# Linear attention with two feed-forward layers: query and key projections of the first eight head pairs as one group of half-row products

## Chip, cores, metric

The kernel runs on one core of a Trainium2 chip. The metric is device time in microseconds of one execution; several executions are taken and the median is given.

## What is computed

Inputs are q, k, v of shape 4 x 8 x 576 x 64 (batch, heads, tokens, head size), a projection w_phi of 64 x 128, and the weights of two feed-forward layers, 512 x 2048 and 2048 x 512 each. All is float32.

```python
def phi(x):
    proj = np.einsum('bhsd,df->bhsf', x, w_phi)
    proj = proj - np.max(np.abs(proj), axis=-1, keepdims=True)
    return np.concatenate([np.exp(proj), np.exp(-proj)], axis=-1)
q_p, k_p = phi(q), phi(k)
kv  = np.einsum('bhsf,bhsd->bhfd', k_p, v)
z   = np.sum(k_p, axis=2)
num = np.einsum('bhsf,bhfd->bhsd', q_p, kv)
den = np.einsum('bhsf,bhf->bhs', q_p, z)[..., None] + 1e-06
x   = (num / den) with heads joined: 2304 x 512
h = x @ w_in;  x = np.maximum(0.01 * h, h) @ w_out
h = x @ w_in2; x = (h / (1 + np.exp(-h))) @ w_out2
```

## The kernel before

Two heads form a pair: 16 pairs, four to a batch entry. The 64 rows of head 0 lie on partitions 0 to 63, those of head 1 on 64 to 127. The first eight pairs (`full(i)`, `NFULL = 8`) multiply in plain float32, which TensorE does in two passes of weight load and matmul for each product; the other eight split each operand into two fp32r parts. The feed-forward layers follow tile by tile, the first in five tiles of 460 or 462 tokens.

The work of one pair is cut into steps, named in `fns` (L365): `lq` and `lv` load (load_qk L109, load_v L119); `pq0`, `pq1` project the two parts of q (s_pq L205: for full pairs 256 and 320 tokens) with the 64 rows of each head as an operand of its own (L217), into one bank for each head; ScalarE copies them to p (L223, L225) and POOL takes the maximum over partitions into m (L227). `pk0`, `pk1` project 512 tokens of k (s_pk L169), each for two blocks of 128 tokens, on all 128 rows against BDF, a block-diagonal matrix that holds w_phi twice and zeros elsewhere (L180), into one bank each; `pkt` does the last 64 tokens (L195). k_features (L151) takes the maximum (L156), subtracts (L157) and forms both exponentials, negative sign first (L166, L167). `eq0`, `eq1` do this for q (L239, L243, L244). `kv` (s_kv L256) sums features times values, 17 products for the positive and then 17 for the negative sign (L262, L268), and ScalarE copies the bank to KV (L273), of which there is one buffer. `num0`, `num1` (num_full L290; products L302, L305) give numerator and denominator, VectorE divides (L311 to L313), TensorE transposes (L316, L320), and put_x (L282) writes x in two parts.

Each step has a due time within its pair (`OFF0` for full pairs, L370); pairs begin 5 units apart. All steps are sorted by due time, and run_att emits them in that order, between the weight preparation and the feed-forward steps (L719 to L769). The tile framework then places the instructions on the engines' queues: it starts from the emitted order and moves instructions by a simulated time line, as operands and buffers come free, so the order in the trace is not the emitted one. Each engine's queue runs in order.

PSUM has eight banks, four with the tag a and four with the tag y. While the first stage is emitted, the steps pq (two banks each), kv and the transposes take y banks, the others a banks (aps, L61). p, m and qh have two buffers each; a pair uses both, one for each part of q.

The preparation of the feed-forward weights (narrow64, L414) is VectorE and ScalarE work on tiles `raw`, three buffers, loaded on SP's queue (L411) as are q, k and v. The third to twelfth of these loads wait for a token (L409) that POOL writes after the maximum of `pq1` of a given pair (L229, PACE L68). w_phi is loaded by two transfers on ScalarE's queue into wc (L75): first BDF, then wraw (w_phi on both row halves) and the identity.

Of the kernel before, what the change touches and what calls it, by code (L numbers as in the profile page):

```python
# [8 lines left out]
F32 = mybir.dt.float32  # L9
# [10 lines left out]
def tile_linear_attention_ffn_ffn(ctx: ExitStack, tc: tile.TileContext, q, k, v, w_phi, w_in1, w_out1, w_in2, w_out2, out):  # L20


    nc = tc.nc
    B, H, S, D = 4, 8, 576, 64
    F = (w_phi.shape[1] - 128) // 3
# [5 lines left out]
    S0 = 512  # L31
# [6 lines left out]
    NKV, NNUM = 112, 96  # L38
# [5 lines left out]
    gp = ctx.enter_context(tc.tile_pool(name="gp", bufs=2))  # L44
# [7 lines left out]
    def at(shape, dt, tag):  # L52
        return att_pool[0].tile(shape, dt, tag=tag, bufs=AB[0].get(tag, 1), name=tag)

    def ps(tag):

        return psp.tile([128, 512], F32, tag=tag, name=f"ps_{tag}")
# [3 lines left out]
    def aps(step):  # L61

        return ps("y" if PRO[0] and step in ("pq", "kv", "nt") else "a")
# [3 lines left out]
    BDF, wraw, ident = wc[:, 0 : 2 * F].rearrange("p (j f) -> p j f", j=2), wc[:, 2 * F : 3 * F], wc[:, 3 * F :]  # L67
# [5 lines left out]
    def make_consts():  # L73
        for c in (slice(0, 2 * F), slice(2 * F, 3 * F + 128)):
            nc.scalar.dma_start(wc[:, c], w_phi[:, c])  # L75
        first = [const.tile([128, 2], F32, name=f"first{i}") for i in range(2)]
        nc.gpsimd.memset(first[0], 0.0)
        nc.gpsimd.partition_all_reduce(first[1], first[0], 128, bass_isa.ReduceOp.absmax)
# [30 lines left out]
    def load_qk(i):  # L109

        st = P[i]
        st["kr"] = at([128, S0], F32, "kr")
        st["kt"] = at([128, 128], F32, "kt")
        st["qr"] = at([128, S], F32, "qr")
        nc.sync.dma_start(st["kr"], k[i, :, 0:S0])
        nc.sync.dma_start(st["kt"], k[i, :, S0:])
        nc.sync.dma_start(st["qr"], q[i])

# [6 lines left out]
    def sub(out_, x, h):  # L125
        nc.vector.tensor_tensor(out_, x, h.bitcast(F32), op=ALU.subtract)  # L126

    def full(i):
        return i < NFULL
# [21 lines left out]
    def k_features(i, pk, ng, g0):  # L151

        ke = P[i]["ke"]
        km = at([128, 4], F32, "km")
        src = pk[:, 0 : ng * F].rearrange("p (g f) -> p g f", f=F)
        nc.vector.tensor_reduce(km[:, 0:ng], src, op=ALU.max, axis=AX.X, apply_absolute_value=True)  # L156
        nc.vector.tensor_tensor(  # L157
            ke[:, g0 : g0 + ng, 0, :], src, km[:, 0:ng].unsqueeze(2).to_broadcast([128, ng, F]), op=ALU.subtract
        )
        g1 = g0 + ng  # L160
        if g1 == 8:
            return
        if g1 == 9:
            g0 = 4
        e0, e1 = ke[:, g0:g1, 0, :], ke[:, g0:g1, 1, :]
        nc.scalar.activation(e1, e0, AF.Exp, scale=-1.0)  # L166
        nc.scalar.activation(e0, e0, AF.Exp)  # L167

    def s_pk(c2):  # L169
        def f(i):  # L170
            st = P[i]
            if c2 == 0:
                st["ke"] = at([128, 9, 2, F], F32, "ke")
            pk = aps("pk")
            for u in range(2):
                c = 2 * c2 + u
                cs = slice(c * 128, (c + 1) * 128)
                o = pk[:, u * 2 * F : (u + 1) * 2 * F]
                if full(i):
                    nc.tensor.matmul(o, st["kr"][:, cs], BDF.rearrange("p j f -> p (j f)"), start=True, stop=True)  # L180
                    continue
                bh, bl = BDH.rearrange("p j f -> p (j f)"), BDL.rearrange("p j f -> p (j f)")
                nc.tensor.matmul(o, st["krh"][:, cs], bh, start=True, stop=False)
                nc.tensor.matmul(o, st["krl"][:, cs], bh, start=False, stop=False)
                nc.tensor.matmul(o, st["krh"][:, cs], bl, start=False, stop=True)
            k_features(i, pk, 4, 4 * c2)

        return f
# [16 lines left out]
    def s_pq(a):  # L205

        def f(i):
            st = P[i]
            c0, n = part(i, a)
            p = at([128, 2 * n], F32, "p")  # L210
            st["p", a] = p
            pq = [aps("pq"), aps("pq")]
            cs = slice(c0, c0 + n)
            for j in range(2):
                if full(i):
                    r = slice(64 * j, 64 * j + 64)
                    nc.tensor.matmul(pq[j][:, 0:n], wraw[r], st["qr"][r, cs], start=True, stop=True)  # L217
                    continue
                nc.tensor.matmul(pq[j][:, 0:n], WH, st["qs"][:, j, cs], start=True, stop=False)
                nc.tensor.matmul(pq[j][:, 0:n], BDL[:, j], st["qs"][:, j, cs], start=False, stop=True)  # L220
            for j in range(2):
                w = 256 if full(i) else n
                nc.scalar.activation(p[:, j * w : (j + 1) * w], pq[j][:, 0:w], AF.Copy)  # L223
                if w < n:
                    nc.scalar.activation(p[:, 512 + 64 * j : 576 + 64 * j], pq[j][:, w:n], AF.Copy)  # L225
            m = at([128, 2 * n], F32, "m")
            nc.gpsimd.partition_all_reduce(m, p, 128, bass_isa.ReduceOp.absmax)  # L227
            if a == 1 and full(i):
                nc.gpsimd.tensor_copy(token[:, i : i + 1], m[0:1, 0:1])  # L229
            st["m", a] = m  # L230

        return f
# [23 lines left out]
    def s_kv(i):  # L256
        st = P[i]
        ke, va = st["ke"], st["va"]
        pv = aps("kv")[:, 0 : 4 * NKV].rearrange("p (s j d) -> p s j d", s=2, j=2)
        vf = va.rearrange("p c d -> p (c d)")  # L260
        for s in range(2):
            nc.tensor.matmul(  # L262
                pv[:, s, :, 0 : D + 1], ke[:, 8, s, :], va[:, 8:10], start=True, stop=False, skip_group_check=True
            )
            for j in range(2):
                for c in range(4):
                    w = (4 * j + c) * (D + 1)
                    nc.tensor.matmul(  # L268
                        pv[:, s, j], ke[:, 2 * c + j, s, :], vf[:, w : w + NKV], start=False, stop=(j == 1 and c == 3), skip_group_check=True
                    )  # L270
        if full(i):
            st["KV"] = at([128, 2, 2, NNUM], F32, "KV")
            nc.scalar.activation(st["KV"], pv[:, :, :, 0 : NNUM], AF.Copy)  # L273
            return
        h, l = st["KVH"], st["KVL"] = at([128, 2, 2, 2, D], F32R, "KVH"), at([128, 2, 2, 2, D], F32R, "KVL")
        for j in range(2):
            kv_, z_ = pv[:, :, j, 0:D], pv[:, :, j, D : D + 1].to_broadcast([128, 2, D])
            for slot, sr in ((j, kv_), (1 - j, z_)):
                nc.scalar.activation(h[:, j, :, slot, :], sr, AF.Copy)
                sub(l[:, j, :, slot, :], sr, h[:, j, :, slot, :])  # L280
# [68 lines left out]
    def s_fin(a):  # L349
        def f(i):  # L350
            if full(i):
                return
            st = P[i]
            c0, w = part(i, a)
            x = st["x", a]
            nc.vector.tensor_mul(x, x, st["r", a])
            put_x(i, slice(0, 128), x, c0, w)

        return f

    def s_num(a):
        return lambda i: (num_full if full(i) else num_split)(i, a)

    W, WP = 8.0, 5.0
    fns = dict(  # L365
        lq=load_qk, lv=load_v, sp=s_split, pq0=s_pq(0), pq1=s_pq(1),
        pk0=s_pk(0), pk1=s_pk(1), pkt=s_pkt, eq0=s_eq(0), eq1=s_eq(1), kv=s_kv, num0=s_num(0), num1=s_num(1), fin0=s_fin(0), fin1=s_fin(1),
    )
    FIN = 16
    OFF0 = dict(lq=1.1, lv=3.08, sp=3.09, pq0=4.48, pk0=5.33, pk1=5.331, pq1=6.8, eq0=9, pkt=9.13, kv=9.131, num0=11.3, eq1=12.07, num1=16, fin0=11.3001, fin1=16.0001)  # L370
    OFF1 = dict(lv=0.6, lq=-2.1250, sp=0.5, pq0=2.1172, pk0=4.0606, pk1=4.0616, pq1=4.7479, eq0=6.2094, pkt=5.1, kv=8.3898, num0=12.1423, eq1=13.9119, num1=14.457, fin0=FIN, fin1=FIN + 2.3)
    END0 = max(OFF0.values()) + 1
    END1 = max(OFF1.values()) + 1
    ts = [WP * i for i in range(NFULL)]
    ts += [ts[-1] + END0 - min(OFF1.values()) + W * i for i in range(B * HP - NFULL)]
    seq = sorted(((ts[i] + o, i, n) for i in range(B * HP) for n, o in (OFF0 if full(i) else OFF1).items()))
    seq.reverse()
# [337 lines left out]
    def pace(s):  # L715

        return SLOW * min(s, NC) + FAST * max(0, s - NC)

    make_consts()  # L719
    for c in range(PRE):  # L720
        run_att(13.52 + 11.07 * c)
        prep_wi(0, c)
# [52 lines left out]
    for u, gs in GROUPS.items():  # L775
        for i, ps_ in enumerate(gs):
# [7 lines left out]
            if last:  # L784
                y = y3_ops(u, list(ps_))
# [87 lines left out]
```

## Time and profile before

| | |
|---|---|
| median of 3 executions | 964.19 us (962.32 to 964.91) |
| the profiled execution | 963.19 us |
| its span, first to last instruction | 961.4 us |
| PE (TensorE matmuls) busy | 943.6 us, 98% |
| DVE (VectorE) busy | 649.1 us, 68% |
| ACT (ScalarE) busy | 597.2 us, 62% |
| POOL (GpSimd) busy | 78.4 us, 8% |
| transferred | 226.13 MB, 235 GB/s on the mean |

PE is the matmul, PEld the weight load that overlaps it. The end of a matmul is modelled, so groups of matmuls overlap in a listing; the time a group takes of PE is read from its start to the start of the next group. L180 is line 180 of the kernel. "idle before <- releaser" names what ended an engine's idle time.

### The profile page before, as it was taken

The numbers are of one execution on the slowest core, as the hardware profiler recorded it, in microseconds if no ns is written. First come the engines' busy times: TensorE is split into PE (matmuls) and PEld (weight loads), VectorE is DVE, ScalarE is ACT, GpSimd is POOL, SyncE is SP. The second block draws the span as 40 slices with busy tenths as digits, with TensorE's granted clock in tenths as the row PEclk, the third lists the DMA queues.
The fourth block names the chain that finished last, engine by engine and source line by source line (L and its number), as shares of the span: only waits on it lengthen the run. The fifth ranks groups of instructions, "written<-read, shape, count | busy, mean of one in ns | idle before, by whom it ended". The sixth has DMA issues, their size and how long they took to land.

```text
span 961.4 us, 15778 instructions
## 1 busy us (share of the span) xinstructions
PE 943.6 (98%) x5376; PEld 883.6 (92%) x5376; DVE 649.1 (68%) x1279; ACT 597.2 (62%) x1224; POOL 78.4 (8%) x56
## 2 busy tenths in 40 slices
PE   7999999999999999999999999999999999999998
PEld 6878888889999998888888999999999999999998
DVE  6677799986666655278777767778762595624853
ACT  6568687877777776466655556566554565544553
POOL 3434200201111111000000000000000000000000
PEclk9999999999999999999999999999999999999999
DMA  6333477874334232299999999896988778987784
GB/s 223 99 105 102 154 243 256 284 267 129 116 112 116 78 128 79 86 355 384 356 337 334 368 356 346 299 349 239 319 287 294 243 234 264 300 281 222 251 278 138
DMA packets 102384, 226.13 MB, mean 235 GB/s; under 512 B 15008, under 2 KB 24992, under 8 KB 102304
## 3 DMA queue, kind: packets, MB, share of 16 engines
q1 hardware_dynamic: 102016, 224.86, 69.9%
q8 instruction: 43, 0.70, 0.3%
q14 instruction: 37, 0.30, 0.1%
q10 hardware_dynamic: 288, 0.26, 0.1%
HBM read 177.82 MB, written 47.22 MB: 234 GB/s over the span
## 4 chain that ended last, share of the span: by engine, by line
PE 79%; DMA 8%; DVE 6%; ACT 4%; issue 1%; SPq 1%; DVEq 0%; ACTq 0%
PE ps_y L689 18%; PE ps_y L553 16%; PE ps_a L533 16%; PE ps_a L613 10%; PE ps_y L613 8%; DMA d<-rec 2%; PE ps_a L268 2%; PE ps_a L302 2%; DMA rec<-e 2%; PE ps_a L334 1%; PE ps_y L268 1%; DMA raw<-in_moe_w_in_dram 1%; DMA e<-d 1%; PE ps_a L180 1%; DMA w7s<-wst 1%
## 5 line engine op out<-in xcount | busy, mean ns | idle before, releaser
L689 PE MATMUL ps_y<-gt,ws 128*128 128x384 f32 x1008 | 177.2, 337 | 0.0
L689 PEld LDWEIGHTS ps_y<-gt,ws 128*128 128x128 f32 x1008 | 176.4, 188 | 0.1
L553 PE MATMUL ps_y<-gh,wo 128*128 128x460 f32 (+1 forms) x640 | 149.5, 372 | 2.2 <-DVE wo L126 1.3
L553 PEld LDWEIGHTS ps_y<-gh,wo 128*128 128x128 f32 x640 | 119.0, 188 | 16.6 <-ACT gh L429 1.9
L533 PE MATMUL ps_a<-xh,wih 128*128 128x460 f32 (+1 forms) x320 | 119.4, 373 | 0.8 <-ACT p L223 0.8
L533 PE MATMUL ps_a<-xl,wih 128*128 128x460 f32 (+1 forms) x320 | 118.9, 372 | 0.0
L533 PE MATMUL ps_a<-xh,wil 128*128 128x460 f32 (+1 forms) x320 | 118.7, 371 | 0.0
L613 PE MATMUL ps_a<-xs,ws 128*128 128x384 f32 x546 | 104.7, 338 | 0.1
L613 PEld LDWEIGHTS ps_a<-xs,ws 128*128 128x128 f32 x546 | 96.7, 188 | 0.8 <-issue 0.4
L227 POOL PARTITION_ALL_REDUCE m<-p x32 | 72.9, 2280 | 293.7 <-ACT p L223 212.4
L429 ACT ACTIVATE gt<-g 128x384 fp32r<-128x384 f32 x120 | 62.8, 524 | 51.3 <-PE ps_y L689 49.3
L126 DVE TENSOR_TENSOR gt<-g,gt 128x384 fp32r<-128x384 f32 x120 | 66.5, 555 | 34.4 <-ACT gt L429 33.5
L613 PE MATMUL ps_y<-xs,ws 128*128 128x384 f32 x462 | 88.5, 338 | 0.1
L613 PEld LDWEIGHTS ps_y<-xs,ws 128*128 128x128 f32 x462 | 81.7, 188 | 0.6 <-DVE g L589 0.5
L553 PE MATMUL ps_y<-gl,wo 128*128 128x460 f32 (+1 forms) x320 | 81.6, 372 | 0.0
L126 DVE TENSOR_TENSOR gl<-g,gh 128x460 fp32r<-128x460 f32 (+1 forms) x80 | 51.6, 646 | 30.6 <-ACT gh L429 26.1
L533 PEld LDWEIGHTS ps_a<-xh,wih 128*128 128x128 f32 x320 | 60.2, 188 | 7.4 <-ACT p L223 1.0
L553 PEld LDWEIGHTS ps_y<-gl,wo 128*128 128x128 f32 x320 | 60.2, 188 | 7.0
L536 ACT ACTIVATE g<-ps_a 128x460 f32<-128x460 f32 (+1 forms) x80 | 44.1, 552 | 35.9 <-PE ps_a L533 35.1
L533 PEld LDWEIGHTS ps_a<-xh,wil 128*128 128x128 f32 x320 | 60.1, 188 | 6.8
L533 PEld LDWEIGHTS ps_a<-xl,wih 128*128 128x128 f32 x320 | 60.2, 188 | 6.0
L429 ACT ACTIVATE gh<-g 128x460 fp32r<-128x460 f32 (+1 forms) x80 | 46.6, 584 | 8.1 <-PE ps_y L553 7.1
(142 smaller groups left out, 1552.3 us busy)
## 6 DMA issues: line engine op xcount, KB each, us to landing
ws<-w7s SPq DMA_DIRECT2D x336, 256.0 KB, 3.7
wo<-wos SPq DMA_DIRECT2D x64, 512.0 KB, 5.2
w7s<-wst SPq DMA_DIRECT2D x48, 512.0 KB, 6.0
raw<-in_moe_w_in_dram SPq DMA_DIRECT2D x32, 512.0 KB, 5.3
raw<-in_moe_w_out_dram SPq DMA_DIRECT2D x32, 512.0 KB, 5.8
wos<-wo SPq DMA_DIRECT2D x16, 512.0 KB, 4.3
va<-in_v_dram SPq DMA_DIRECT2D x16, 325.0 KB, 4.1
qr<-in_q_dram SPq DMA_DIRECT2D x16, 288.0 KB, 3.9
```

Source lines behind the costliest of these rows:

```text
L126: nc.vector.tensor_tensor(out_, x, h.bitcast(F32), op=ALU.subtract)
L180: nc.tensor.matmul(o, st["kr"][:, cs], BDF.rearrange("p j f -> p (j f)"), start=True, stop=True)
L227: nc.gpsimd.partition_all_reduce(m, p, 128, bass_isa.ReduceOp.absmax)
L268: nc.tensor.matmul(pv[:, s, j], ke[:, 2 * c + j, s, :], vf[:, w : w + NKV], start=False, stop=(j == 1 and c == 3), skip_group_check=True)
L302: nc.tensor.matmul(pb[:, w : w + NNUM], e[:, s, cs], KV[:, s, j], start=(s == 0), stop=(s == 1))
L334: nc.tensor.matmul(o, lhs, st[m, a][:, s, j * w : (j + 1) * w], start=(n == 0), stop=(n == 5))
L429: nc.scalar.activation(h, f, AF.Copy)
L533: nc.tensor.matmul(ph, a[:, kk, :], b_[:, kk, :], start=(m == 0), stop=(m == 3 * KD - 1))
L536: nc.scalar.activation(g, ph, AF.Prelu, alpha=0.01)
L553: nc.tensor.matmul(Y[t][d][:, 0:n], a[:, ds_], b_, start=(c == 0 and m == 0), stop=(c == NC - 1 and m == 1), skip_group_check=True)
L613: nc.tensor.matmul(bank[b_], w[:, a, kk], x[:, c, kk], start=(first and m == 0), stop=(m == 5), skip_group_check=True)
L689: nc.tensor.matmul(bank[b_][db], w[:, a, db], t[:, c], start=(first and p == 0 and m == 0), stop=(p == NP - 1 and m == 2), skip_group_chec ...
```

## The change

For full pairs, pk0 forms the whole k product of 512 tokens: for each block of 128 tokens and each head, 64 rows of kr against 64 rows of wraw, one bank for each head; pk1 does nothing. The feature groups of ke are therefore ordered by head, then block, and kv reads them so. kv takes the negative sign first, in all pairs. pq0, pq1 and pk0 of a full pair are due right after one another, pq1 being due 2.3 units earlier and the k product 0.85 earlier than before. The first pair's kr is loaded by two transfers. At the very start, behind a memset on VectorE, TensorE multiplies zeros by zeros three times, 256 columns in float32, into a y bank that nobody reads.

```diff
@@ load_qk
-        nc.sync.dma_start(st["kr"], k[i, :, 0:S0])
+        for c in (slice(0, 256), slice(256, S0)) if i == 0 else (slice(0, S0),):
+            nc.sync.dma_start(st["kr"][:, c], k[i, :, c])
@@ s_pk
+            if full(i):
+                if c2 == 0:
+                    pks = [aps("pk"), aps("pk")]
+                    for c in range(4):
+                        for j in range(2):
+                            r = slice(64 * j, 64 * j + 64)
+                            nc.tensor.matmul(
+                                pks[j][:, c * F : (c + 1) * F], st["kr"][r, c * 128 : (c + 1) * 128], wraw[r], start=True, stop=True
+                            )
+                    for j in range(2):
+                        k_features(i, pks[j], 4, 4 * j)
+                return
             pk = aps("pk")
...
-                if full(i):
-                    nc.tensor.matmul(o, st["kr"][:, cs], BDF.rearrange("p j f -> p (j f)"), start=True, stop=True)
-                    continue
@@ s_kv
-        for s in range(2):
+        for s in (1, 0):
...
+                    g = 4 * j + c if full(i) else 2 * c + j
                     nc.tensor.matmul(
-                        pv[:, s, j], ke[:, 2 * c + j, s, :], vf[:, w : w + NKV], start=False, stop=(j == 1 and c == 3), skip_group_check=True
+                        pv[:, s, j], ke[:, g, s, :], vf[:, w : w + NKV], start=False, stop=(j == 1 and c == 3), skip_group_check=True
                     )
@@ due times
-    OFF0 = dict(lq=1.1, lv=3.08, sp=3.09, pq0=4.48, pk0=5.33, pk1=5.331, pq1=6.8, eq0=9, pkt=9.13, kv=9.131, num0=11.3, eq1=12.07, num1=16, fin0=11.3001, fin1=16.0001)
+    OFF0 = dict(lq=1.1, lv=3.08, sp=3.09, pq0=4.48, pk0=4.482, pk1=4.483, pq1=4.481, eq0=9, pkt=9.13, kv=9.131, num0=11.3, eq1=12.07, num1=16, fin0=11.3001, fin1=16.0001)
@@ start
+    def wake():
+
+        z, bank = gp.tile([128, 256], F32, tag="g", name="z", bufs=2), ps("y")
+        nc.vector.memset(z, 0.0)
+        for _ in range(3):
+            nc.tensor.matmul(bank[:, 0:256], z[:, 0:128], z, start=True, stop=True)
+
     make_consts()
+    wake()
```

## Rows read from the trace of the kernel before

**Rows 1.** The page, busy us, share of the span and instructions of each engine.

```profile
PE 943.6 (98%) x5376; PEld 883.6 (92%) x5376; DVE 649.1 (68%) x1279; ACT 597.2 (62%) x1224; POOL 78.4 (8%) x56
```

**Rows 2.** Busy us by stretch: PE, PEld, DVE, ACT, POOL; then granted clock, DMA.

```profile
0.00:5.00 5.00, 0.69 (x2) 0.61 (x3) 0.27 (x1) 1.97 (x3) 0.66 (x6) 1.00 0.67 199
60.00:111.00 51.00, 49.33 (x389) 42.88 (x389) 42.15 (x96) 38.47 (x88) 20.56 (x18) 1.00 0.30 102
111.00:120.00 9.00, 9.00 (x49) 8.11 (x49) 3.90 (x11) 5.33 (x10) 0.00 (x0) 1.00 0.67 233
120.00:180.00 60.00, 60.00 (x304) 53.78 (x303) 57.44 (x113) 47.45 (x88) 2.55 (x1) 1.00 0.83 266
180.00:200.00 20.00, 17.30 (x87) 14.87 (x86) 19.78 (x36) 17.71 (x34) 3.04 (x1) 1.00 0.63 216
```

**Rows 3.** The chain of waits from 60 to 111 us, shares by line.

```profile
by line: DVE r L425 8.7%; DMA raw<-in_moe_w_in_dram 8.5%; PE ps_a L302 8.3%; DVE t L424 8.0%; DMA raw<-in_moe_w_out_dram 7.5%; DVE ke L157 6.1%; issue 6.0%; DVE km L156 5.9%; DVE t L422 5.4%; DVE x L313 4.1%; ACT t L420 3.8%; DVE t L423 3.3
```

**Rows 4.** PE in order of time, 33 to 41 us: start, us, what.

```profile
33.42 1.89 PE L180 MATMUL ps_a<-wc,kr 128*128 128x256 f32 x8
35.15 0.38 PE L316 MATMUL ps_y<-wc,x 128*128 128x128 f32 x2
35.46 0.81 PE L217 MATMUL ps_y<-qr,wc 64*128 64x320 f32 x4
36.20 0.49 PE L262 MATMUL ps_y<-va,ke 128*128 128x130 f32 x2
36.52 1.94 PE L268 MATMUL ps_y<-va,ke 128*128 128x112 f32 x16
38.30 0.40 PE L262 MATMUL ps_y<-va,ke 128*128 128x130 f32 x2
38.53 1.94 PE L268 MATMUL ps_y<-va,ke 128*128 128x112 f32 x16
40.40 0.70 PE L217 MATMUL ps_y<-qr,wc 64*128 64x256 f32 x4
```

**Rows 5.** Weight loads of L217: over all (min/median/max ns), and around 30 us.

```profile
L217 PEld LDWEIGHTS ps_y<-qr,wc x64: 182/186/238, 8.4 to 103.9; 64*128 64x128 f32 x64
...
30.04 0.30 PEld L217 LDWEIGHTS ps_y<-qr,wc 64*128 64x128 f32 x4
```

**Rows 6.** PE in order of time, the first 10 us.

```profile
4.30 3.78 PE L180 MATMUL ps_a<-wc,kr 128*128 128x256 f32 x8 [4.30 <-DMA wc<-in_w_phi_dram]
7.88 0.64 PE L195 MATMUL ps_a<-wc,kt 128*128 128x128 f32 x2
...
9.67 0.70 PE L180 MATMUL ps_a<-wc,kr 128*128 128x256 f32 x2
```

**Rows 7.** Transfers of wc and, in the first 10 us, qr: issues, first and last; landing.

```profile
L75 ACTq DMA_DIRECT2D wc<-in_w_phi_dram x2: 403/430/457, 0.7 to 1.2; - x2
...
DMA to landing us min/median/max: 3.5/3.6/3.6
...
L117 SPq DMA_DIRECT2D qr<-in_q_dram x3: 328/432/662, 1.6 to 5.6; - x3
...
DMA to landing us min/median/max: 3.8/4.9/5.4
```

**Rows 8.** What PE waited for: us in total, times, longest.

```profile
PE ps_a L262 <- ACT ke L167: 0.9, 2, 0.6
...
PE ps_y L262 <- ACT ke L167: 0.8, 2, 0.4
```

**Rows 9.** ACT and PE in order of time, around 44 us.

```profile
43.57 0.49 ACT L273 ACTIVATE KV<-ps_y 128x384 f32<-128x384 f32 x1 [1.55 <-PE ps_a L305]
...
44.11 2.02 PE L302 MATMUL ps_a<-KV,qh 128*128 128x96 f32 x16 [0.58 <-ACT KV L273]
```

**Rows 10.** The page's groups: POOL's reduction; busy, mean ns, idle before, releaser.

```profile
L227 POOL PARTITION_ALL_REDUCE m<-p x32 | 72.9, 2280 | 293.7 <-ACT p L223 212.4
```

**Rows 11.** The chain of waits from 111 us on: the first piece of the feed-forward layer.

```profile
111.96 5.10 PE ps_a L533 x24
```

## The prediction

> **What bounds the kernel now.** I read the busy times of the profile's page first, then the busy time by stretch, the chain of waits, and TensorE's instructions in order of time. It shows PE busy for 943.6 of 961.4 us [rows 1]: time taken off PE is time off the kernel, unless another engine holds the stretch where it is taken. The change touches only the first stage, the eight "full" pairs, so I read by stretch [rows 2]. From 60 to 111 us PE is busy 49.3 of 51 us, VectorE 42.2, ScalarE 38.5. From 120 to 180 PE is busy throughout and VectorE for 57.4 of 60; in 180 to 200 VectorE 19.8 of 20 and PE 17.3. So PE leads the first stage with VectorE some 15% behind; later both are full. A warning stands in the chain from 60 to 111 us [rows 3]: its largest shares are VectorE lines and weight transfers (8 to 9% each), PE's largest is 8.3%. PE is full there, but the order in which VectorE, ScalarE and the queue serve it matters as much.
>
> **The pairs 1 to 7.** An fp32 product runs as two passes of weight load plus matmul. The k product (L180) takes eight passes of 256 columns from 33.42 to 35.15, 1.73 us, so 0.216 us each [rows 4]. Half of these columns multiply the zeros of BDF. The change replaces them by 16 passes of 64 rows and 128 columns, two at a time on the two row halves: eight rounds. A round moves half the columns (0.108 us); its floor is the weight load. The nearest row is L268, 16 passes of 112 columns with a 128-column load each from 36.52 to 38.30, 0.111 us a pass [rows 4]. Eight rounds at 0.111 are 0.89 us: **0.84 us saved** a pair.
>
> That needs the two halves' loads to run side by side. The query projection shows it: its four loads last 0.182 us or more each and all end within 0.30 us [rows 5]; one after another, 0.111 apart, the fourth would only begin at 0.33. The Trainium skill (TensorE: Matmul & The Clock Gate, section LDWEIGHTS) speaks against the change here: a load costs by its columns, so that "A 32×128 weight load takes the same time as a 128×128 weight load"; by that alone 16 loads cost twice eight and nothing is saved. The trace agrees on the cost of one load and shows the overlap that takes the doubling back.
>
> The grouping saves the turns between full and half rows. Leaving: pq1 runs from 35.46 to 36.20, 0.74 us, of which two rounds of 320 columns are 0.54, so 0.20 is idle; the next two passes (L262) take 0.32 against 0.24 at 38.30, 0.08 more. Entering: 16 L268 passes up to L217 take 1.87 us (38.53 to 40.40), up to L262 1.77, 0.10 more [rows 4]. One turn in and out costs 0.38 us; two groups become one: **0.38 us saved** a pair. Together 1.22 us, times seven pairs: 8.5 us. If the group falls apart, with k alone among full-row work, k's own turn eats 0.38 of its 0.84, and 0.46 a pair is left: 3.2 us.
>
> **Pair 0 and the start.** The first k product runs from 4.30 to 7.88, eight passes at 0.45 on average against 0.216 later [rows 4, 6]. The granted clock reads 1.00 in every stretch I read [rows 2], but this doubling is what the half level, 1.2 GHz, would give, after PE had done nothing for 4.3 us. Then come kt and the query halves; the next k product begins at 9.67 [rows 6]. The change puts six zero passes first: at 0.45 us 2.7 us of PE, which was idle until 4.30, behind a memset that no row shows: between nothing and the 0.49 us of a whole copy such as L273's [rows 9]. They end before or about when data lands: I cost them at nothing, with 0.3 us as the other end. What they gain is the clock: nothing if it rises when it did, the whole doubling if earlier. The k product now waits for wraw, the second half of wc: issued at 1.15, 3.6 to land, so 4.75 instead of 4.30. qr follows on SP behind one more kr issue (some 0.45 us): 1.62 + 0.45 + 3.8, about 5.9 [rows 7]. The group lasts 1.9 us at full clock, 3.8 at half, kt 0.25 to 0.57. The end, 9.67 before, becomes 7.2 at best (query part after qr, 1.0, and kt) and 10.3 at worst: 2.5 us gained to 0.6 lost. I take 1.0, because the pairs' features on VectorE and ScalarE stand between this and the next PE work. The extra issue moves the queue's later loads by 0.45 us; kt, qr and va are waited for by PE work behind the k product, and the third kr load waits for that product anyway, so I cost it at nothing beyond this.
>
> **The rest.** Negative sign first in kv: the first L262 needs L166's result instead of L167's, which follows it on ScalarE (0.6 us). PE waits 0.8 us in full pairs and 0.9 in later ones for L167 [rows 8]. Zero to 1.7; I take 1.0. The reordered groups of ke change nothing: reductions, subtractions and exponentials keep number and size, and both banks are full 0.89 us after the start, when the first one was before.
>
> **What is given back.** pq1 beside pq0 needs four of the four y banks while kv of the pair before holds one until ScalarE copies it (L273). That copy itself waits for PE's num work; PE then idled 0.58 us for it [rows 9]. Bounds: nothing (the k passes need no y bank and can run between) to 0.58 a pair. I take 0.18, 1.3 us over seven pairs. And half of the last four pairs' saving (4 x 1.22 / 2 = 2.4 us) for the chain of rows 3. Sum: 8.5 + 1.0 + 1.0 - 1.3 - 2.4 = 6.8 us. The profiled execution took 963.19 us (span 961.4 and 1.8 around it), the median of the runs shown is 964.19, 1.0 above. 963.2 - 6.8 + 1.0 gives **957.4 us**. What follows should move along: weight loads are released by tokens that come after pq1, which is earlier in its pair, and from 111 to 120 us VectorE is busy only 3.9 of 9 [rows 2], so the preparation that fills it from 120 on can start earlier too. If that slack comes on top, up to 5 us more: 952.
>
> **Rivals.** (1) VectorE and ScalarE hold the first stage from 60 us: for it speaks the chain [rows 3], against it that VectorE has 8.8 us free there. Then the last four pairs give nothing and the full bank wait takes 4.1: 8.5 - 4.9 + 2.0 - 4.1 = 1.5 us, 962.7: within 0.3%. 13%. (2) The group is formed in the program but torn by waits for banks: 3.2 + 2.0 - 1.3 = 3.9, 960.3. 13%. (3) The loads of the two halves queue: the k product keeps its 1.73, the turns give 0.38 x 7 = 2.7, with 2.0 less 1.3: 3.4 us, 960.8. The loads seen [rows 5] speak against. 4%. (The rule cited above, from the Trainium skill's page TensorE: Matmul & The Clock Gate, would come to this.) (4) **Slower**: pq1's copies. Each pair's two halves fill both buffers of p, and a copy of the next pair's pq1 can go only when VectorE has subtracted the maxima of this pair's second half, which POOL makes in 2.28 us each [rows 10]. Placed earlier, the copy may stand at the head of ScalarE's queue and hold the exponentials behind it, which kv waits for. It decides when it costs PE more than 10.5 / 7 = 1.5 us a pair; a whole reduction is 2.28, so 7 x 2.28 - 10.5 = 5.5 us slower, 969.7. Against it: eq1 needs only its reduction, which comes earlier too. 10%. (5) The change does nothing to speak of because the instructions are put in another order by the kernel's planner and the query halves stay apart: as (2).
>
> **How the numbers follow.** The forecast has 60%: nearly all of the PE saving, with some of it returned; its own range is 952 to 961. A measurement of this kernel tells about 0.3%, 2.9 us, from no change: faster means below 961.3. The forecast, (2) and (3) lie below it: 60 + 13 + 4 = 77%; (1) is the 13% within, (4) the 10% slower. The range 952 to 963.8 takes in forecast and rivals 1 to 3 and leaves the slow case and the tails.
>
> **What would show it.** Eight rounds of the k product in 0.9 us in the listing of TensorE's instructions, directly behind the query halves, with one turn per pair; half-clock passes only before some 6 us; FFN passes (L533) beginning some 6 us before 111.96 [rows 11]; then the same work in the same time. Wrong would be: k rounds of 0.2 us; a wait of PE for p, KV or xh in each pair of over half a microsecond; VectorE at 95% before 100 us; or an earlier L533 whose lead is lost between 120 and 200 us, where VectorE is full.

## The result: 0.65% slower, and the profile after

The changed kernel takes 969.71 us (median of 4, 969.19 to 972.31) against 964.25 beside it: 1.0065 times as long, interval [1.0042, 1.0089]. That is 5.5 us slower, where 6.8 us faster was forecast. Its profiled execution took 970.1 us, span 968.3, so 6.9 us above the one of before. In the listings of the new kernel's lines the k product is L181, kt's L205, the query halves L227, kv L272 and L279, num L313 and L316, the transposes L327 and L331, the first feed-forward product L544.

The page's busy times:

```profile
PE 948.9 (98%) x5446; PEld 892.4 (92%) x5446; DVE 652.2 (67%) x1280; ACT 596.9 (62%) x1224; POOL 77.1 (8%) x56
```

TensorE (PE) has 70 passes more and is busy 5.3 us longer than in [rows 1], though the half-row passes should have cut it. The stretch from 60 to 111 us shows where (columns as in [rows 2]; the number behind POOL's is the granted clock):

```profile
60.00:111.00 51.00, 45.39 (x370) 40.13 (x368) 40.39 (x79) 33.45 (x78) 21.28 (x17) 0.97 0.31 99
```

PE is busy 45.4 instead of 49.3 us there and does not get further for it, and the clock is below 1.00. The first pass of the feed-forward layer, which began at 111.75, begins at 120.97: the whole loss, and 2.3 us more that come back later, lies in the first stage.

```profile
120.97 0.46 PE L544 MATMUL ps_a<-xh,wih 128*128 128x462 f32 x1
```

Cutting that stage at each change of the granted clock gives the account of the 9.2 us:

```profile
10.50:24.15 13.65, 11.02 (x92) 9.27 (x90) 11.68 (x23) 10.57 (x24) 5.73 (x4) 1.00 0.63 219
24.15:30.98 6.83, 6.83 (x34) 6.76 (x33) 4.66 (x10) 3.84 (x8) 2.69 (x3) 0.50 0.27 77
30.98:95.83 64.85, 58.94 (x504) 51.86 (x504) 48.57 (x101) 44.23 (x102) 26.19 (x22) 1.00 0.33 99
95.83:99.24 3.41, 3.41 (x18) 3.41 (x18) 3.41 (x8) 0.72 (x1) 0.00 (x0) 0.50 0.84 297
99.24:112.90 13.66, 11.35 (x94) 10.12 (x93) 10.20 (x23) 10.15 (x24) 5.45 (x5) 1.00 0.12 45
112.90:116.30 3.40, 3.40 (x18) 3.40 (x17) 3.40 (x10) 2.54 (x5) 0.00 (x0) 0.50 0.27 51
116.30:120.97 4.67, 4.57 (x42) 4.27 (x42) 1.28 (x3) 2.03 (x5) 0.00 (x0) 1.00 1.01 389
```

These are 110.47 us, PE busy 99.52 and idle 10.95. Nearly the same work before:

```profile
10.50:111.75 101.25, 95.92 (x737) 82.92 (x735) 79.90 (x171) 72.87 (x164) 41.67 (x34) 1.00 0.36 115
```

That one has 5.33 idle and no half level. In the changed kernel 13.64 busy us ran at the half level, 1.2 GHz; an estimate at the full level, 2.4 GHz, is half of it, 6.82. So the 9.2 us are 6.8 of half clock, plus 5.6 more idle, less 3.2 of work really saved (92.7 against 95.9).

What PE waited for up to 111 us, with total, times and longest:

```profile
PE ps_a L313 <- DVE ke L158: 3.8, 2, 2.5
PE ps_a L313 <- DVE wil L127: 2.2, 1, 2.2
PE ps_y L327 <- DVE x L324: 1.7, 1, 1.7
```

The wait ahead of the first half-level stretch, and two ahead of the third, which end behind that window:

```profile
23.83 0.46 PE L313 MATMUL ps_a<-KV,qh 128*128 128x96 f32 x2 [2.25 <-DVE wil L127]
111.81 0.41 PE L327 MATMUL ps_y<-wc,x 128*128 128x128 f32 x2 [1.84 <-DVE x L324]
112.68 0.62 PE L272 MATMUL ps_y<-va,ke 128*128 128x130 f32 x2 [0.46 <-ACT ke L167]
```

The long waits are new; before, the longest after the start was 1.2 us. The first two half-level stretches begin 0.3 and 0.7 us after PE's return from waits of 2.25 and 2.49 us. The third begins 0.2 us after the wait of 0.46 us, which follows the one of 1.84. Behind the other two waits of over a microsecond (1.33 us to 41.24, 1.67 to 80.19) there is none. The wait ahead of 95.83, TensorE and then VectorE (DVE) and POOL in order of time:

```profile
91.50 1.16 PE L181 MATMUL ps_a<-wc,kr 64*128 64x128 f32 x16
95.16 2.66 PE L313 MATMUL ps_a<-KV,qh 128*128 128x96 f32 x14 [2.49 <-DVE ke L158]
```

```profile
92.15 1.57 DVE L433 TENSOR_SCALAR t<-t 128x512 f32<-128x512 f32 x1
...
94.07 0.75 DVE L434 TENSOR_SCALAR t<-t 128x512 uint32<-128x512 uint32 x1
94.74 0.27 DVE L158 TENSOR_TENSOR ke<-ps_a,km 128x128 f32<-128x128 f32 x1
```

```profile
89.62 4.92 POOL L237 PARTITION_ALL_REDUCE m<-p  x2 [9.68 <-DVE t L434]
```

num (L313) waits for an a bank, and the bank that comes free is kt's, once VectorE has subtracted its maxima (L158). That takes 0.27 us, but weight preparation (L433, L434) stands ahead of it in VectorE's queue, and one piece of it (L433) takes 1.57 us where its kind mostly takes 0.42. It lies beside POOL's maxima: with pq1 due beside pq0, the two maxima of a pair run back to back, 89.62 to 94.54 here and likewise ahead of 80.19 and 111.81, while in the kernel before they stood apart (86.65 to 88.59 and 93.11 to 95.85). No run isolates what that alone costs. Nothing here is half rows being slow. PE in a pair of the changed kernel:

```profile
35.17 0.80 PE L227 MATMUL ps_y<-qr,wc 64*128 64x320 f32 x2
35.90 0.44 PE L327 MATMUL ps_y<-wc,x 128*128 128x128 f32 x2
36.27 0.33 PE L331 MATMUL ps_y<-wc,x 64*64 64x64 f32 x4
36.53 2.02 PE L313 MATMUL ps_a<-KV,qh 128*128 128x96 f32 x16
38.40 0.41 PE L205 MATMUL ps_a<-wc,kt 128*128 128x128 f32 x2
38.74 1.16 PE L181 MATMUL ps_a<-wc,kr 64*128 64x128 f32 x16
```

Compare [rows 4]: the k product follows num and kt's product, 3.6 us behind the last query passes. In this pair one head's passes of pq1 stand here and the other's ahead of kv; from 47.86 us on pq0 and pq1 lie together, with num still between them and the k product. The group of half-row passes that names the change is not formed in these pairs; at the start, one k product follows the query halves of pair 0 (9.32 us), as it did before (9.67).

### The profile page after: what moved, and what is told of

Same layout as the page of the kernel before. It is cut to its first block, busy times and chain, and to the rows that moved or that the text cites. A ratio compares the mean times of both kernels' runs of the same rounds, so it can differ in the third digit from the quotient of the medians.

```text
span 968.3 us, 15922 instructions
## 1 busy us (share of the span) xinstructions
PE 948.9 (98%) x5446; PEld 892.4 (92%) x5446; DVE 652.2 (67%) x1280; ACT 596.9 (62%) x1224; POOL 77.1 (8%) x56
## 4 chain that ended last, share of the span: by engine, by line
PE 77%; DMA 7%; DVE 6%; ACT 4%; issue 3%; POOL 1%; SPq 1%; ACTq 0%; DVEq 0%; POOLq 0%
PE ps_y L700 18%; PE ps_a L544 16%; PE ps_y L564 16%; PE ps_a L624 10%; PE ps_y L624 8%; PE ps_a L279 2%; DMA d<-rec 2%; DMA rec<-e 2%; PE ps_y L279 1%; PE ps_a L345 1%; DMA raw<-in_moe_w_out_dram 1%; POOL m L237 1%; PE ps_a L313 1%; DMA w7s<-wst 1%; DVE t L433 1%
## 5 line engine op out<-in xcount | busy, mean ns | idle before, releaser
L544 PE MATMUL ps_a<-xh,wih 128*128 128x460 f32 (+1 forms) x320 | 119.3, 373 | 0.7 <-ACT g L547 0.7
L544 PE MATMUL ps_a<-xl,wih 128*128 128x460 f32 (+1 forms) x320 | 119.0, 372 | 0.0
L544 PE MATMUL ps_a<-xh,wil 128*128 128x460 f32 (+1 forms) x320 | 118.9, 372 | 0.0
L544 PEld LDWEIGHTS ps_a<-xh,wih 128*128 128x128 f32 x320 | 60.2, 188 | 7.2 <-ACT g L547 0.9
L544 PEld LDWEIGHTS ps_a<-xh,wil 128*128 128x128 f32 x320 | 60.2, 188 | 6.8
L544 PEld LDWEIGHTS ps_a<-xl,wih 128*128 128x128 f32 x320 | 60.3, 188 | 6.1
```

Source lines behind the costliest of these rows:

```text
L544: nc.tensor.matmul(ph, a[:, kk, :], b_[:, kk, :], start=(m == 0), stop=(m == 3 * KD - 1))
```

## Experiments

Eighteen kernels ran. Ratios are to the kernel before on the same chip (median 962.85 to 964.12), with their 95% interval. Where an edit is given against the kernel before, everything else is unchanged.

**The parts one at a time.** First the half-row k product alone:

```diff
+            if full(i):
+                if c2 == 0:
+                    pks = [aps("pk"), aps("pk")]
...
+                            nc.tensor.matmul(pks[j][:, c * F : (c + 1) * F], st["kr"][r, c * 128 : (c + 1) * 128], wraw[r], start=True, stop=True)
```

> The kernel before with one edit: the k product of the full pairs in 16 half-row passes (with the order of the feature groups that belongs to it). Due times, signs and start as before. Theory A (the loss comes from pq1 being put beside pq0: both reductions of POOL and the copies of both parts fall into one stretch, and the PE work that covered the features of k is gone): the half-row passes by themselves save, 957 to 962 us, and the first feed-forward pass begins at 105 to 110 us instead of 111.75. Rival R1 (the half-row product itself costs: both k banks are complete at once, and num has to wait for one of them): 967 to 971, first feed-forward pass at 117 to 122 us. Rival R2 (VectorE and ScalarE hold the stage, PE's saving is not used, nor is anything lost): 963 to 966.

982.94 us, ratio 1.0209 [1.0177, 1.0242], the worst of the parts and worse than the whole change.

The due times alone:

```diff
-    OFF0 = dict(... pk0=5.33, pk1=5.331, pq1=6.8, ...)
+    OFF0 = dict(... pk0=4.482, pk1=4.483, pq1=4.481, ...)
```

> The kernel before with one edit: the due times of the change (pq1, pk0, pk1 right behind pq0). The k product stays on full rows. Theory A: this is where the loss sits, 967 to 973 us, first feed-forward pass at 116 to 122 us, both reductions of a pair back to back on POOL. Rival R1: 963 to 966, as before. Rival R2: 963 to 966.

968.33 us, 1.0056 [1.0034, 1.0077].

The zero products alone:

```diff
+    wake()
```

> The kernel before with one edit: the three zero products at the start. All theories: the first k product runs at full clock some microseconds earlier, its last pass and the pair's query parts end 0.5 to 2 us earlier than 9.67; the whole 962.5 to 964.5 us, as the next waits (features, weight tiles) take most of it. If the zero products disturb the order instead (an extra y bank at the start), 965 to 968.

962.82 us, 0.9989 [0.998, 0.9999]: a microsecond, or nothing.

The change with pq1 due at its old place:

```diff
-    OFF0 = dict(... pq1=4.481, ...)
+    OFF0 = dict(... pq1=6.8, ...)
```

> The changed kernel with one edit: pq1 due at 6.8 again, as before. Half-row k product, negative sign first, zero products and the split first load stay. Theory A: 956 to 961 us, first feed-forward pass at 104 to 110 us. Rival R1 (half-row product): 967 to 971. Rival R3 (the sign order or the start makes the loss): 967 to 971 here, and 957 to 965 in the run with half rows alone.

977.43 us, 1.0128 [1.0099, 1.0156]. Moving pq1 back makes it worse, so pq1 beside pq0, the forecast's slower rival, is not by itself the loss; e4's order is another one again. Of the parts only the zero products come out near their cost; the traces of e1, e2 and e4 show other work in other places on all queues.

**Length and place of the k product.** e1 with two more full-row products in each full pair, which the half-row passes then overwrite:

```diff
+                    for j in range(2):
+                        nc.tensor.matmul(pks[j][:, 0 : 2 * F], st["kr"][:, 0:128], BDF.rearrange("p j f -> p (j f)"), start=True, stop=True)
```

> The run with half rows alone (982.9 us), with four full-row passes of 256 columns put in front of each pair's half-row passes; their results are overwritten. PE's time for the k product is then 0.86 + 0.89 = 1.75 us as before, plus a turn of 0.38. Theory B (half rows lose because PE, having less to do, waits longer in single stretches for VectorE and ScalarE; after waits of 2 us and more the granted clock falls to half for 3.4 to 13.7 us, and everything is late once more): with the work back, 963 to 971 us, at most one half-clock stretch before the feed-forward layer. Rival R4 (half-row passes as such lower the clock or cost turns): 978 to 988, with half-clock stretches as in the run without the padding. Rival R5 (the padding only adds PE time): 985 to 995.

972.67 us, 1.0092 [1.0064, 1.012]. More work on PE, and 10 us less than e1.

The other way round, a k product shortened with full rows: only the first head's, on 128 columns, its features used for both.

```diff
-                    nc.tensor.matmul(o, st["kr"][:, cs], BDF.rearrange("p j f -> p (j f)"), start=True, stop=True)
+                    nc.tensor.matmul(pk[:, u * F : (u + 1) * F], st["kr"][:, cs], BDF[:, 0], start=True, stop=True)
```

> The kernel before, with the k product of the full pairs computed for one head of the two alone: 8 passes of 128 columns on all 128 rows, 0.9 us instead of 1.73; the features read each column twice, so that VectorE and ScalarE do what they did. No half rows, no turns, no new bank. What it leaves out: the k features of the second head. Theory B (shorter PE work, longer waits, then a lower clock): slower or no better than before, 964 to 980 us, with half-clock stretches that the kernel before does not have. Rival R4 (half rows as such): 956 to 961, since the same PE time is saved without them. Rival R1 (both banks of k complete together): 956 to 961, for the banks are complete one after the other here.

972.78 us, 1.0095 [1.0077, 1.0114]: half the columns and no half rows cost 9.9 us as well.

The changed kernel with kv in an a bank, so that the y banks hold no group back:

```diff
-        return ps("y" if PRO[0] and step in ("pq", "kv", "nt") else "a")
+        return ps("y" if PRO[0] and step in ("pq", "nt") else "a")
```

> The changed kernel with one edit: kv takes an a bank instead of a y bank in the first stage. Each pair then has the k passes directly behind pq1's, which the changed kernel does not have (there, num and kt lie between). Theory B: the grouping is not what decides; PE still waits where it has nothing to cover with; 963 to 975 us. Rival R6 (the change fails only because its group is never formed, for want of y banks): 954 to 961 us.

988.48 us, 1.0258 [1.024, 1.0277]. Here k passes do come right behind or between the passes of pq1, as the change intends, and PE waits 10.4 us in all for KV and 7.9 for x.

The negative sign first alone:

```diff
-        for s in range(2):
+        for s in (1, 0):
```

> The kernel before with one edit: the negative sign first in kv. Both theories: PE's waits for L167 at L262, 1.7 us in all, go; 962 to 964.5 us, the same within the measurement. If another order of instructions follows from it, up to 3 us to either side.

967.85 us, 1.005 [1.0031, 1.0068]. Two loops swapped cost 5 us, 2.0 of them up to the first feed-forward pass (113.71); the queues of VectorE and ScalarE came out in another order. That led to the next runs.

**The order held fixed.** The framework orders the queues by its own simulated time line. For these runs the order of every queue is written down as numbers and imposed by edges between neighbours of one engine, which add no wait:

```diff
+    for numbers in queues.values():
+        for first, then in zip(numbers, numbers[1:]):
+            tc.add_manual_dep(tc.nc.find_inst_by_name(f"I-{then}"), f"I-{first}", info, reason="queue order")
```

The short full-row product of e6 in the order of before:

> The shortened full-row product (k features of the second head left out), with every engine's queue held to the order of the kernel before by ordering edges that add no waits. Theory O (what costs is the order of the instructions on the queues, which the planner's simulated time line makes anew when a product has another length or place): 954 to 961 us, first feed-forward pass at 104 to 109, no half-clock stretch before it. Theory B (less PE work means longer waits for VectorE and ScalarE whatever the order, and those lower the clock): 964 to 975, like the 972.8 of the run without the edges.

962.82 us, 1.001 [0.9991, 1.0029]: the 9.9 us of e6 are gone.

The half-row product of e1 in the order of before:

> The half-row product alone (982.9 us in the planner's own order), with every queue held to the order of the kernel before; the two half-row products of a block stand where its full-row product stood. Theory O: 955 to 963 us, first feed-forward pass at 104 to 111. Theory B: 967 to 985, with half-clock stretches. Rival R4 (half rows as such): 967 to 985 here, while the short full rows in the old order are at 954 to 961.

964.72 us, 1.0021 [1.0005, 1.0036]: of e1's 18.8 us, 1.5 are left.

The kernel before, its work unchanged, in the order of e1:

> The kernel before, all its work unchanged, with every queue held to the order that the run with half rows alone had. Theory O: 972 to 990 us, as slow as that run or slower, since PE has more to do. Theory B: 962 to 968, for the work is the one of before.

980.77 us, 1.018 [1.0163, 1.0197]: the order alone makes 17.6 us. Up to 130 us its clock is 0.95 and PE is busy 110.95:

```profile
0.00:130.00 130.00, 110.95 (x765) 96.03 (x766) 84.52 (x182) 79.68 (x176) 40.21 (x40) 0.95 0.38 123
```

The whole change but its due times, in the order of before:

> The changed kernel without its due times: half-row product, negative sign first, zero products, split first load, with every queue held to the order of the kernel before (the zero products first on PE, the second part of the first load behind the first). Theory O: 953 to 962 us, no slower than the half rows in the old order; faster than both kernels of the case. Theory B: 967 to 985.

963.64 us, 1.0016 [1.0001, 1.0031]. So e9, e10 and e12 lose next to nothing, but each lies above the range that theory O gave it: the order makes the loss, and the shorter work in the old order makes no gain. The edges by themselves cost nothing that shows: e15 and e17, below, are old work in the old order, at 1.0007 and 0.9998.

**The changed kernel's own order.** The work of before, negative sign first and with the due times of the change, in the order of the changed kernel:

> The kernel before with the full-row k product and without zero products or the split load, negative sign first, every queue in the order of the changed kernel. Theory O (the order alone makes the loss): within 2 us of the changed kernel's 969.7 or above it, since the old k product costs 0.84 us more in each pair. If half rows, zero products or the split load have a cost of their own in the changed kernel: clearly below it, 963 to 966.

969.42 us, 1.0058 [1.0044, 1.0073]: the loss of the change, without half rows, zero products or the split load. Its waits up to 111 us are of the same kind as the changed kernel's, VectorE's x and ke foremost:

```profile
PE ps_y L316 <- DVE x L313: 2.9, 2, 1.8
PE ps_a L302 <- DVE ke L157: 2.7, 2, 2.0
PE ps_a L302 <- DVE wil L126: 1.1, 1, 1.1
```

**Why the old order does not gain either.** GpSimd (POOL) takes 2.3 us for each maximum, with VectorE slower beside it. In these two the reduction covers 16 columns; the maxima of the others are left out:

```diff
-            nc.gpsimd.partition_all_reduce(m, p, 128, bass_isa.ReduceOp.absmax)
+            w = slice(2 * n - 16, 2 * n) if full(i) else slice(0, 2 * n)
+            nc.gpsimd.partition_all_reduce(m[:, w], p[:, w], 128, bass_isa.ReduceOp.absmax)
```

> Half-row k product in the order of before, and GpSimd's maxima of the eight full pairs taken over the last 16 columns only (left out: the other columns' maxima; one column's maximum is subtracted everywhere). Theory V (the time that half rows free on PE turns into waits because GpSimd's 2.3 us reductions, and VectorE slowed beside them, hold the first stage): 955 to 959, and clearly below the next kernel. Rival E (the chain of features, exponentials and copies on VectorE and ScalarE holds it, whatever GpSimd does): 962 to 965, as with whole maxima.

> The kernel before in its own order with the same short maxima and the full-row k product. Theory V: 960 to 963, between the kernel before and the half-row kernel, since PE is full in this one. Rival E: 962 to 965, no difference from before or from the half-row kernel with short maxima.

962.58 us, 0.9993 [0.998, 1.0007], and 963.75 us, 1.0007 [0.9997, 1.0017]. With half rows the feed-forward layer began at 109.6 us, 2.2 before that of the kernel before. The lead was still 1.9 at the 241st of the 960 passes of its first product (238.3 against 240.2 us), but two thirds of it was lost by the 481st (397.8 against 398.5). With the old work (e15) the layer began at 113.9, after a half-level stretch of 3.4 us at 20 us. Theory V asked for 955 to 959 and falls: POOL's time holds part of the first stage, not the kernel.

The next three follow the largest wait of e10 (x, 1.66 us near 90). There VectorE stood at a weight that had just landed, with the reciprocal and x queued behind. First the token that releases the transfers is written earlier, with half rows and then without:

```diff
-            if a == 1 and full(i):
+            if a == 0 and full(i):
                 nc.gpsimd.tensor_copy(token[:, i : i + 1], m[0:1, 0:1])
```

> Half-row k product in the order of before, but the token that releases the weight transfers is written after the maximum of pq0 of the same pair instead of pq1's, and POOL's copies that use it come right behind it (some 6 us earlier in each pair); the other four queues keep the order of before. Theory T (each pair waits for a weight transfer: it starts after pq1's maximum, ScalarE and VectorE stand at its preparation, and the reciprocal and x that PE's transposes need are queued behind it, so shorter k products only lengthen PE's wait): the PE waits for x and KV fall from 5.2 us to under 3, the feed-forward layer begins 2 to 5 us before 112.6, and the time is 958 to 962. Rival C (the chain of num, d, x, xh, kv and KV itself holds the stage, the transfer is covered): PE waits as before, 963 to 966.

> The kernel before in its own order with the same early token. Theory T: PE is full here apart from some 5 us of waits, so 1 to 3 us faster than before at most, 960 to 963, and slower than the half-row kernel with the early token. Rival C: no difference from before, 962 to 965.

965.34 us, 1.003 [1.002, 1.004], and 962.79 us, 0.9998 [0.999, 1.0007]. In e16 the token of that pair came at 76.34 us, but the load was issued at 84.72, since a store (84.30) stood ahead of it on SP's queue and waited for VectorE. So the last one also moves that store behind the two loads:

> The half-row kernel with the early token, and on SP's queue the first store of a finished weight moved behind the two weight loads that stood after it: in the run before, the token came at 76.34 us but the loads were issued at 84.72, behind that store, which waited 11.4 us for VectorE. Theory T (this late weight makes ScalarE, VectorE and, through x, PE wait): the loads are issued near 77 us, the 2.05 us wait of PE for x near 91 us is gone, the feed-forward layer begins 1.5 to 2.5 us before 112.7, and the time is 962 to 964. Rival C (another link of the chain of num, x, kv and KV takes the same place): the first layer begins at 112 to 113 and the time stays at 964.5 to 966.

964.62 us, 1.0012 [1.0001, 1.0022]. The loads went out at 76.71 and 77.20, and the wait near 90 us fell to 0.72. A wait for x of 1.02 us appeared at 99.05 where e10 had none:

```profile
99.05 0.44 PE L327 MATMUL ps_y<-wc,x 128*128 128x128 f32 x2 [1.02 <-DVE x L324]
```

The feed-forward layer began at 112.3 us (112.6 in e10). Theory T is right about that wait and wrong about the time; rival C holds.

## Why the prediction was wrong, step by step

**Half-row passes: right.** "Eight rounds at 0.111 are 0.89 us" is what the trace shows: the sixteen weight loads and the passes over them run as forecast.

```profile
38.74 0.97 PEld L181 LDWEIGHTS ps_a<-wc,kr 64*128 64x128 f32 x16
```

Each load lasts 0.188 us and starts together with that of the other head. Sixteen full-row loads, of 0.192 us each, took 1.87 us in the kernel before:

```profile
36.41 1.87 PEld L268 LDWEIGHTS ps_y<-va,ke 128*128 128x128 f32 x16
```

The sentence of the Trainium skill (TensorE: Matmul & The Clock Gate, section LDWEIGHTS) that a 32-row load takes as long as a 128-row one agrees with the single loads (0.188 and 0.192 us); the doubling that the prediction drew from it does not occur here. Rival 3 is out.

**"Two groups become one": wrong.** The due times ask for it, the order that comes out does not have it, and two turns a pair remain. Rival 5 said so, but priced only the torn group (960.3), not what else moves with it.

**That the order of before stays: the step that failed.** It was never written as a step. Every sum took PE's passes out of the sequence of [rows 4] and left the neighbours where they were; what a new order would do to VectorE and ScalarE stood at nothing, without a reason. e11 and e13 show that the order alone, with the old work, makes the loss of e1 (17.6 of 18.8 us) and of the change (6.2 against 5.5). e9, e10 and e12 show that the new work in the old order moves the median by -0.4 to +1.5 us. In the changed order VectorE's short instructions stand behind weight preparation, PE waits up to 2.5 us at a time, and to 5.6 us more of idle time the half clock adds 6.8.

**"Half of the last four pairs' saving" and 1.3 for banks given back: mis-sized.** In the old order the k product stands alone between full-row work. For that the prediction had 3.2 us over seven pairs, and PE's busy time bears it out: it fell from 943.6 to 939.8 us in e10. All of it goes into waits. PE's waits of the kernel before and then of e10 from 5 to 111 us, apart from the first weights:

```profile
PE ps_a L302 <- ACT KV L273: 2.7, 5, 1.2
PE ps_y L316 <- DVE x L313: 0.8, 1, 0.8
PE ps_y L262 <- ACT ke L167: 0.8, 2, 0.4
PE ps_y L262 <- ACT p L225: 0.6, 1, 0.6
PE ps_a L302 <- ACT wih L429: 0.3, 1, 0.3
```

```profile
PE ps_a L313 <- ACT KV L284: 3.3, 5, 1.3
PE ps_y L272 <- ACT ke L168: 1.9, 3, 1.0
PE ps_y L327 <- DVE x L324: 1.9, 2, 1.7
PE ps_a L313 <- ACT wih L440: 0.9, 1, 0.9
PE ps_y L272 <- ACT p L235: 0.9, 1, 0.9
PE ps_a L313 <- ACT qh L254: 0.2, 1, 0.2
```

Together 5.2 and 9.1 us: 3.8 us off the work, 3.9 onto the waits. It is not the clock: the four executions of e10 with a mean granted clock of 0.999 or more took 962.8 to 965.4 us. One place shows how, the kernel before and then e10:

```profile
87.54 1.89 PE L180 MATMUL ps_a<-wc,kr 128*128 128x256 f32 x8
90.22 0.41 PE L316 MATMUL ps_y<-wc,x 128*128 128x128 f32 x2 [0.80 <-DVE x L313]
```

```profile
88.01 1.16 PE L181 MATMUL ps_a<-wc,kr 64*128 64x128 f32 x16
90.84 0.41 PE L327 MATMUL ps_y<-wc,x 128*128 128x128 f32 x2 [1.66 <-DVE x L324]
```

From the k product to the next transposes it takes 2.68 us with long passes and 2.83 with short ones; the wait grew by 0.86. This is what rival 1 said (13%, 962.7), though of another order; e12 measured 963.64. The 15% that VectorE had free from 60 to 111 us were no cover: PE waits for one given result, and busy shares don't tell when it is ready. What the passes would save as one group, 1.22 us a pair, is not shown: no run had the group in an order that does not lose.

**The start: a gain without its cause.** The zero products were to bring the full clock forward. The trace's first record of the full level begins at 10.50 us in the changed kernel, 9.36 in e3 and 10.29 in e12, against 8.59 before; in the changed kernel the first k product took nearly twice its later time:

```profile
3.04 1.06 PE L735 MATMUL ps_y<-z 128*128 128x256 f32 x2
4.50 2.08 PE L181 MATMUL ps_a<-wc,kr 64*128 64x128 f32 x16 [0.41 <-DMA wc<-in_w_phi_dram]
...
9.32 1.93 PE L181 MATMUL ps_a<-wc,kr 64*128 64x128 f32 x14
```

The next k product begins at 9.32 instead of 9.67: 0.35 us of the 1.0 taken, and not by the clock: the first k product is 1.6 us shorter, and the query parts behind it, before at the full level in part, are 0.9 longer. In e4, with the same start, the full level did come early, at 4.42, and went again at 7.84, as a wait of 1.58 us for qr ended:

```profile
4.43 1.16 PE L181 MATMUL ps_a<-wc,kr 64*128 64x128 f32 x16 [0.33 <-DMA wc<-in_w_phi_dram]
```

**The sign first, +1.0: wrong in sign and in kind.** Alone it costs 5 us (e8), by order. Within the old order, in e12, it costs nothing that can be told from the rest.

**Rival 4** gave 969.7, and 969.71 was measured: that is chance. It had PE waiting for kv's exponentials behind pq1's copies on ScalarE. The waits of the changed kernel are for VectorE's ke, x and wil; none is for p, and the two for exponentials (L167) are of 0.2 and 0.5 us. What pq1 beside pq0 does do in that order is to put the two maxima of a pair back to back.

**Open:** which link of num, x, kv and KV would have to be shortened for half rows to pay, and whether some other order gains what they save. Neither was settled; only e3's interval lies below 1, by a tenth of a per cent.

## What to carry to other kernels

Where a framework orders the queues by simulated durations, a shorter product is a change of order on every engine: compare the two orders first, and run the new work in the old order and the old work in the new one before explaining a time by the work. A saving on a busy engine counts only if the result that its next instruction waits for is also earlier; read that from the pair of rows around it, not from the other engine's busy share.

## What the runs showed of the hardware that was not expected

- **Half-level stretches behind PE's waits.** In the changed kernel waits of 2.2, 2.5 and 1.8 (with 0.5 more) us were followed by half-level stretches of 6.8, 3.4 and 3.4 us; e7 had 13.7 us in one piece. The length of a single wait does not tell whether one follows: behind e16's 2.05 us and e12's 2.62 there is none, while e8 and e15 have one of 3.4 us at 20 us, behind waits of 1.1 and 1.4, and the kernel before, with 1.2 us in the same place, has none. So theory B's "waits of 2 us and more" is not borne out, and what decides is not shown.
- **When the full level first comes scatters.** With zero products it came at 4.42 us (e4), 6.70 (e7), 9.36, 10.29 and 10.50 (e3, e12, changed); without them at 7.74 (e6) to 11.32 (e16). Whether they help is not shown by one trace of each.
- **VectorE slows beside POOL's reductions.** Up to 125 us every VectorE instruction of over 1 us lies beside a reduction, seven in the kernel before and nine in the changed one; with short maxima (e14, e15) there is none. The same preparation step, minimum, median and longest ns, in the kernel before and, as L426, with short maxima (e15):

```profile
L424 DVE SCALAR_TENSOR_TENSOR t<-raw,t x64: 679/685/1602, 15.4 to 618.5; 128x512 uint32<-128x512 uint32 x64
```

```profile
L426 DVE SCALAR_TENSOR_TENSOR t<-raw,t x64: 648/686/694, 16.2 to 619.9; 128x512 uint32<-128x512 uint32 x64
```

  The Trainium skill (GPSIMD Engine Reference, section Key points) says that the two engines share their interfaces to SBUF and contend where a VectorE instruction has two SBUF inputs or runs in a two-port mode. This step has two inputs, and the rows agree, with up to 0.9 us for one instruction. L433 above has one input and was slowed by 1.15; whether it ran in such a mode the trace does not show.
